# Five edits to the schedule of a windowed attention and feed-forward kernel: V's shift, one pair's casts, one pair's mask, the output copies and the last row group

## The chip, the cores and the metric

One core of a Trainium2 chip runs the whole program. The time is what the device needs for one execution, in microseconds (us). The kernel before took 345.44 us as the median of 4 runs (344.41 to 345.81). The core has five engines that run side by side, each with its own instructions in order: PE (matmuls; its weight loads are shown as PEld), DVE (vector work), ACT (activations and copies), POOL (also called GpSimd) and SP, which here only issues DMAs.

## What is computed

```python
def _attn_ref(q, k, v):                       # B, H, S, D = 8, 8, 576, 64
    scores = scale * np.matmul(q, k.transpose(0, 1, 3, 2))
    rel = pos[:, None] - pos[None, :]
    mask = (rel >= 0) & (rel < 64)
    scores = np.where(mask, scores, -1000000000.0)
    ...
    return np.matmul(attn, v)                 # attn: softmax of scores

def _moe_ref(x, w_in, w_out):                 # x: 4608 x 512
    h = x @ w_in                              # 512 x 2048
    g = h - np.tanh(h)
    return g @ w_out                          # 2048 x 512
```

Each query sees itself and the 63 keys ahead of it. The attention's output, with its heads side by side, is the input x of the second part. Inputs and output are float32; the kernel computes with bfloat16 operands and accumulates in float32.

## The kernel before

**Attention.** The 576 positions are cut into 9 windows of 64 queries; window j needs the 128 keys from 64 j - 64 to 64 j + 63. Heads are taken in pairs (h and h + 4), four pairs a batch, 32 pairs in all; pair g belongs to batch g // 4. A pair goes through these steps. Its q and k are loaded from DRAM by POOL's DMAs, rearranged by `cast` (two copies, `cast_pair` does both), transposed on PE (`tr_rows` or `tr`) and moved from PSUM to the tiles `kT` and `qs` or `qT`. `tile_scores` (pairs 0 to 9) or `scores` multiplies them for 5 and 4, or 3, windows at a time, and ACT writes the exponential into `PT`. `tile_pv` or `pv` multiplies with V, and DVE divides by the row sums into `xs`. `x_tr` (PE, then ACT or DVE) or `x_dma` transposes `xs` into `xT`, the operand of the second part.

**The mask** comes in two ways. With "hide", `hides` first adds a large negative number to the masked scores on PE, by a matmul of the identity with the tile `hide` for each head, before the scores are accumulated on top. With "mask", that is left out, and DVE multiplies the exponentials by the 0/1 tile `mask_sb` afterwards (line 278).

**V.** A batch's V is loaded, rearranged into `vb` by four copies (`cast_v`), and spread over the tile `vw` with one window of 64 keys in the upper 64 partitions of each column block: `keys_v`, 9 DMAs of 65 KB, issued in turn from POOL and SP. The lower 64 partitions are the same keys one block on. For the first three batches `shift_dve` copies them with two DVE instructions (line 154), for four blocks each; later ones use DMAs (`windows_v`, which writes a block's 128 keys at once, or `keys_v` with `shift_v`).

**The second part.** Tokens go in 9 chunks of 512. For each of 16 slices m of the hidden width, `hp_mm` does 4 matmuls (line 365, 128 x 512) into a PSUM bank and ACT takes the tanh; `g_sub` subtracts it on DVE into `gT`. For each group of 128 rows, `yp_mm` does 16 matmuls in four parts of four (line 389) into a bank, `y_out` copies the bank to SBUF on ACT (line 394) and issues the output DMA on SP (line 396).

**The order.** It is written out by hand. The last loop runs over half-steps h. `OPS` names the matmul part of a half-step: for chunk 0, slice m stands at h = 2 m; chunk 1 at 32 + 2 m; the output parts of chunk 0 at 64 + m; from h = 80 the slices of a chunk c stand at even h and the output parts of chunk c - 1 at odd h. `items` holds what else is given at a half-step: the attention's steps of the coming batches, in the order of the `at` calls. In a half-step the matmul part is given first, then the items, then `g_sub` of that slice. Every engine takes its instructions in the order in which they are given here.

The output copies are deferred: when a row group's fourth part is done (h = 67, 71, 75, 79, then each eighth odd half-step from 87 on), it is noted in `done`, and `flush` gives the copy and its DMA at the start of the next half-step that has a matmul part, after the items of its own:

```python
        if op:
            flush()
...
            yp_mm(*op[1:])
            if op[2] % 4 == 3:
                done.append((op[1], op[2] // 4))
```

The steps around the change, with the half-steps at which the kernel before gives them: pair 6's casts at 16, pair 7's at 18, both on DVE; pair 6's transposes at 17 and 18, its scores at 20 and 21; pair 7's transposes at 19 and 20, its scores at 23 and 24; batch 1's shift at 21 and its `tile_pv` at 22, 24, 26 and 28. On POOL: batch 2's `cast_v` at 21, its `keys_v`, both halves of w_out, q of batch 3, pair 9's casts, k and v of batch 3 all at 23, in this order, then pair 10's casts at 24 and pair 11's at 38. Pair 8's casts stand at 27 on DVE, its transposes at 29 and 30, its scores at 33 and 35. Batch 2's shift is at 40. Batch 3's V windows are issued at 71, four of them on SP and five on POOL.

PSUM banks: output groups use banks 0 and 1 in chunk 0, bank 2 in chunks 1 to 7, and banks 0 and 2 in turn in chunk 8, the last.

Of the kernel before, what the change touches and what calls it, by code (L numbers as in the profile page):

```python
# [7 lines left out]
F32 = mybir.dt.float32  # L8
BF16 = mybir.dt.bfloat16
ALU = mybir.AluOpType  # L10
ACT = mybir.ActivationFunctionType
# [4 lines left out]
def kernel(  # L16
# [9 lines left out]
    nc = tc.nc  # L26
# [5 lines left out]
    d_model = moe_w_in.shape[0]  # L32
    d_ff = moe_w_in.shape[1]
    NT = B * S
    TOK = 512
    WPC = TOK // 64
    NC = NT // TOK
    M = d_ff // 128
# [9 lines left out]
    sm_pool = ctx.enter_context(tc.tile_pool(name="sm", bufs=3))  # L48
# [6 lines left out]
    ps = psum.tile([128, 8, 512], F32, name="ps")  # L55
# [5 lines left out]
    mask = ps[:, 5, 448:480].bitcast(BF16)  # L61
    hide = const.tile([128, 2, 64], BF16, name="hide")
    WIDE = 1024, 1024
    w_in_sb = [const.tile([128, 4, n], BF16, name=f"wi{i}") for i, n in enumerate(WIDE)]
    w_out_sb = const.tile([128, M, d_model], BF16, name="w_out_sb")
# [76 lines left out]
    def cast_v(b, pr, eng=nc.gpsimd):  # L142
        move(eng, vb[:, :, 2 * pr:2 * pr + 2, 0:D].rearrange("p e h d -> p h e d"),
             stage.pop((b, pr, "v")).rearrange("p h (e d) -> p h e d", d=D))

    def keys_v(b, j, eng=nc.sync):

        eng.dma_start(out=vw[b % 2][64:128, j].rearrange("p h c -> p (h c)"),
                      in_=vb[8 * j:8 * j + 8].rearrange("p e h c -> p e (h c)"))
# [203 lines left out]
    gT = {}  # L353
# [5 lines left out]
    def hp_mm(c, ms, split):  # L359

        outs = [ps[:, hp_bank(c, m), :] for m in ms]
        for kis in ((0, 2), (1, 3)) if split else ((0, 1, 2, 3),):
            for m, hp in zip(ms, outs):
                for ki in kis:
                    nc.tensor.matmul(hp, w_in_tile(ki, m),  # L365
                                     chunk_tile(c)[:, :, ki % 2, 64 * (ki // 2):64 * (ki // 2) + 64],
                                     start=(ki == 0), stop=(ki == 3))
        for m, hp in zip(ms, outs):
            th = sm_pool.tile([128, TOK], F32, tag="th", name="th")
            nc.scalar.activation(th, hp, ACT.Tanh)  # L370
            HID[c, m] = hp, th

    def g_sub(c, m):
        hp, th = HID.pop((c, m))
        if m == 0:
            gT[c] = g_pool.tile([128, M, TOK], BF16, tag="gT", name="gT")
        nc.vector.tensor_tensor(gT[c][:, m, :], hp, th, ALU.subtract)  # L377

    def yp_bank(c, s):
        if c == 0:  # L380
            return s % 2
        return (0, 2)[s % 2] if c == NC - 1 else 2

    def yp_mm(c, st):
        s, part = divmod(st, 4)
        yp = ps[:, yp_bank(c, s), :]
        for i in range(4):
            m = 4 * part + i
            nc.tensor.matmul(yp, gT[c][:, m, s * 128:(s + 1) * 128], w_out_sb[:, m, :],  # L389
                             start=(m == 0), stop=(m == M - 1))  # L390

    def y_out(c, s):
        ysb = sm_pool.tile([128, d_model], F32, tag="ysb", name="ysb")
        nc.scalar.activation(ysb, ps[:, yp_bank(c, s), :], ACT.Copy)  # L394
        r0 = c * TOK + s * 128
        nc.sync.dma_start(out=out[r0:r0 + 128, :], in_=ysb)

    OPS = {}
    for m in range(M):
        OPS[2 * m] = "h", 0, m  # L400
        OPS[32 + 2 * m] = "h", 1, m
        OPS[64 + m] = "y", 0, m
        for c in range(2, NC + 1):
            if c < NC:
                OPS[32 * c + 16 + 2 * m] = "h", c, m
            OPS[32 * c + 17 + 2 * m] = "y", c - 1, m

    items = {}

    def at(h, fn, *args):  # L410
        items.setdefault(h, []).append((fn, args))

    done = []

    def flush():
        if done:
            y_out(*done.pop())

    def pace(h):

        c, m = [OPS[i][1:] for i in range(h) if OPS.get(i, "-")[0] == "h"][-1]
        nc.gpsimd.tensor_copy(tick, gT[c][0:1, m, 0:1])
# [5 lines left out]
    V, A, G, Y = nc.vector, nc.scalar, nc.gpsimd, nc.sync  # L428
# [75 lines left out]
        at(2, load, g, "q", G)  # L504
    at(16, cast_pair, 6, V)
    at(18, cast_pair, 7, V)
    at(21, shift_dve, 1, 0, 4)
    for g, t, ka, qa, a, b, eng in ((4, (10, 11, 13, 14), 6, 7, (4, 5), (6, 7), V),
                                    (5, (13, 14, 15, 15), 2, 3, (4, 5), (6, 7), V),
                                    (6, (17, 18, 20, 21), 2, 3, (4, 5), (4, 5), A),  # L510
                                    (7, (19, 20, 23, 24), 2, 3, (4, 5), (4, 5), A),
                                    (8, (29, 30, 33, 35), 3, 2, (4, 5), (4, 5), A),
                                    (9, (36, 37, 41, 43), 3, 2, (4, 5), (4, 5), A)):
        at(t[0], tr_rows, g, "k", ka, eng)
        at(t[1], tr_rows, g, "q", qa, A)
        at(t[2], tile_scores, g, 0, a, "hide" if g < 8 else "mask")
        at(t[3], tile_scores, g, 1, b, "hide" if g < 8 else "mask")
    for pr in range(NP):
        at(22 + 2 * pr, tile_pv, 4 + pr, (6, 7))
    at(27, x_tr, 1, 0, 0, 4, 3, A)  # L520
# [1 line left out]
    at(30, x_tr, 1, 1, 0, 4, 7, V)  # L522
    at(31, x_tr, 1, 1, 4, 9, 4, A)
    at(21, lambda: [cast_v(2, pr) for pr in range(NP)])
    at(27, cast_pair, 8, V)
    at(23, lambda: [keys_v(2, j, (G, Y)[j % 2]) for j in range(NJ)])
    at(23, load_w_out, 0)
    at(23, load_w_out, 1)
    at(23, load_all, 3, "q")
# [17 lines left out]
    for g in range(2 * NP + 2, B * NP):  # L547
        b, pr = divmod(g, NP)
        a = STEPS[b][pr] if b in STEPS else 8 * g - 36
# [34 lines left out]

    for h in range(32 * NC + 64):
        op = OPS.get(h)
        if op:
            flush()
        if op and op[0] == "h":
            c, m = op[1:]  # L590
            if c == 0 and m == 0:
                hp_mm(c, (0, 1, 2), True)
            elif c > 0 or m > 2:
                hp_mm(c, (m,), m == 0)
        elif op:
            yp_mm(*op[1:])
            if op[2] % 4 == 3:
                done.append((op[1], op[2] // 4))
        for fn, args in items.pop(h, []):
            fn(*args)  # L600
        if op and op[0] == "h":
            g_sub(*op[1:])
    flush()
    assert not items

# [28 lines left out]
```

The softmax here doesn't subtract the row's maximum and nothing guards it: scores larger than these inputs give would overflow.

## Time and profile before

| what | value |
|---|---|
| time of the profiled execution | 345.44 us |
| its span (first to last instruction) | 343.4 us |
| median of 4 runs | 345.44 us (344.41 to 345.81) |
| mean clock granted to PE | 0.970 of full speed |
| output matmuls (line 389) | 576, 144.2 us busy |
| slices' matmuls (line 365) | 576, 149.0 us busy |
| gT on DVE (line 377) | 144, 690 ns each |
| tanh on ACT (line 370) | 144, 599 ns each |
| output copies on ACT (line 394) | 36, 599 ns each |
| q and k casts on POOL (line 84) | 46, 855 and 833 ns mean |
| DMA bytes moved | 38.31 MB, mean 112 GB/s |

How to read it. Times are in us from the first instruction of one profiled execution unless marked ns. A row of a timeline gives start, length, engine, line of the kernel, operation, what it writes and reads with its shape, how many instructions were merged, and in brackets how long the engine stood idle just before and what ended that. A row of waits gives who waited for whom: total, times, longest. A row of stretches gives the window, its length, and for PE, PEld, DVE, ACT and POOL the busy time and number of instructions, then PE's granted clock, the busy share of the DMA engines, and GB/s. Matmuls are pipelined and their ends are modelled, so a busy PE need not be PE at its peak.

### The profile page before, as it was taken

To read this page: it belongs to the slowest core of one execution; us is meant where nothing else is said; L and a number is where in the kernel's file an instruction comes from. 1 tells how busy PE (TensorE), PEld (TensorE's weight loads), DVE (VectorE), ACT (ScalarE), POOL (GpSimd) and SP (SyncE) were. 2 spreads that over 40 slices of the span, in tenths; PEclk is the share of its full clock that TensorE was granted. 3 is DMA by queue.
4 is the path that set the end of the run, shared out by engine and by line. 5 is a ranking of instruction groups with operands and counts; after the bars stand their busy time and mean duration, and the time that the engine had idled before them with its cause. 6 is when DMAs were issued, how large, how long until landed. Compare 5 with 4: busy or idle time off the path is not lost.

```text
span 343.4 us, 6300 instructions
## 1 busy us (share of the span) xinstructions
PE 322.7 (94%) x2468; PEld 178.2 (52%) x2468; DVE 199.8 (58%) x330; ACT 188.7 (55%) x344; POOL 109.9 (32%) x158
## 2 busy tenths in 40 slices
PE   6687899889999999999999999999999999999995
PEld 2553555445555555655555555555555444444442
DVE  4476668877236766657676766666665444444300
ACT  3433787666366566666565666666653444444411
POOL 8933479603930815630823196100000000000000
PEclk9558999999999999999999999999999999999999
DMA  8999997993798289648694895433003200100021
GB/s 159 163 173 179 167 177 113 188 197 56 129 189 177 33 158 150 126 76 155 127 171 107 150 174 111 100 86 77 33 31 79 84 31 31 63 31 31 32 90 63
DMA packets 41245, 38.31 MB, mean 112 GB/s; under 512 B 13504, under 2 KB 34496, under 8 KB 41024
## 3 DMA queue, kind: packets, MB, share of 16 engines
q0 software_dynamic: 21296, 19.67, 38.6%
q1 hardware_dynamic: 19568, 17.82, 20.2%
q10 hardware_dynamic: 352, 0.43, 0.4%
q8 instruction: 19, 0.31, 0.4%
q14 instruction: 10, 0.08, 0.1%
HBM read 36.70 MB, written 9.44 MB: 134 GB/s over the span
## 4 chain that ended last, share of the span: by engine, by line
PE 76%; DMA 9%; DVE 7%; ACT 4%; POOL 2%; issue 2%; POOLq 0%; DVEq 0%; ACTq 0%
PE ps L389 36%; PE ps L365 29%; DMA vall<-in_v_dram 5%; PE ps L315 3%; PE ps L299 3%; PE ps L232 3%; DMA vw<-vb 2%; DVE gT L377 2%; DMA kall<-in_k_dram 2%; DVE xs L326 1%; DVE qt L84 1%; ACT ysb L394 1%; ACT qt L82 1%; POOL vall L126 1%; ACT th L370 1%
## 5 line engine op out<-in xcount | busy, mean ns | idle before, releaser
L365 PE MATMUL ps<-xT,wi 128*128 128x512 bf16 x576 | 149.0, 382 | 4.6 <-DVE gT L377 4.0
L389 PE MATMUL ps<-w_out_sb,gT 128*128 128x512 bf16 x576 | 144.2, 379 | 1.5 <-ACT ysb L394 1.5
L377 DVE TENSOR_TENSOR gT<-ps,th 128x512 bf16<-128x512 f32 x144 | 98.8, 690 | 76.7 <-ACT th L370 74.9
L370 ACT ACTIVATE th<-ps 128x512 f32<-128x512 f32 x144 | 86.0, 599 | 86.3 <-PE ps L365 83.2
L365 PEld LDWEIGHTS <-wi 128*128 128x128 bf16 x576 | 60.8, 114 | 51.2 <-issue 8.4
L389 PEld LDWEIGHTS <-gT 128*128 128x128 bf16 x576 | 53.4, 98 | 55.0 <-issue 2.8
L301 ACT ACTIVATE pt<-ps 128x384 bf16<-128x384 f32 x66 | 32.4, 491 | 24.6 <-PE ps L299 24.6
L84 POOL COPY vb<-vall 72x1024 bf16<-72x1024 bf16 x24 | 24.8, 1055 | 38.8 <-DMA vall<-in_v_dram 38.8
L326 DVE TENSOR_TENSOR xs<-ps,rc 64x576 bf16<-64x576 f32 x44 | 33.2, 755 | 1.1
L394 ACT ACTIVATE ysb<-ps 128x512 f32<-128x512 f32 x36 | 21.6, 599 | 18.2 <-PE ps L389 18.2
L84 DVE COPY qt<-ps 64x576 bf16<-64x576 bf16 x22 | 16.7, 760 | 25.4 <-ACT qt L82 25.3
L84 POOL COPY qb<-qall 96x768 bf16<-96x768 bf16 x23 | 19.7, 855 | 26.7 <-DMA qall<-in_q_dram 10.9
L315 PEld LDWEIGHTS <-pt 128*128 128x128 bf16 x198 | 16.6, 98 | 14.7
L315 PE MATMUL ps<-vw,pt 128*128 128x130 bf16 x198 | 22.0, 220 | 0.0
L299 PE MATMUL ps<-qt,kt 128*128 128x128 bf16 x198 | 21.8, 219 | 0.0
L299 PEld LDWEIGHTS <-kt 128*128 128x128 bf16 x198 | 15.4, 98 | 8.9 <-issue 0.3
L84 POOL COPY kb<-kall 96x768 bf16<-96x768 bf16 x23 | 19.1, 833 | 2.4 <-PE ps L232 2.4
L82 ACT ACTIVATE kt<-ps 128x576 bf16<-128x576 bf16 x26 | 16.9, 651 | 1.6 <-PE ps L232 1.5
L305 DVE TENSOR_TENSOR pt<-pt,ps 128x1152 bf16<-128x1152 bf16 x22 | 16.4, 745 | 0.8 <-ACT pt L301 0.8
L274 ACT ACTIVATE pt<-ps 128x640 bf16<-128x640 f32 (+1 forms) x20 | 12.5, 648 | 4.9 <-PE ps L271 4.8
L82 ACT ACTIVATE qt<-ps 64x576 bf16<-64x576 bf16 x22 | 14.0, 636 | 1.1 <-PE ps L232 1.1
L82 ACT ACTIVATE xT<-ps 128x512 bf16<-128x512 bf16 (+3 forms) x18 | 7.3, 456 | 8.3 <-PE ps L332 8.3
(72 smaller groups left out, 200.8 us busy)
## 6 DMA issues: line engine op xcount, KB each, us to landing
out_dram<-ysb SPq DMA_DIRECT2D x36, 256.0 KB
vall<-in_v_dram POOLq DMA_DIRECT2D x7, 576.0 KB, 13.0
qall<-in_q_dram POOLq DMA_DIRECT2D x5, 576.0 KB, 10.1
kall<-in_k_dram POOLq DMA_DIRECT2D x5, 576.0 KB, 10.2
vw<-vb SPq DMA_DIRECT2D x38, 65.0 KB
wi<-in_moe_w_in_dram POOLq DMA_DIRECT2D x2, 1024.0 KB, 16.5
w_out_sb<-in_moe_w_out_dram POOLq DMA_DIRECT2D x2, 1024.0 KB, 13.8
kall<-in_k_dram POOLq DMA_DIRECT2D x11, 144.0 KB, 7.6
```

The costliest lines, as they stand in the source:

```text
L82: nc.scalar.activation(o, i, ACT.Copy)
L84: eng.tensor_copy(o, i)
L299: nc.tensor.matmul(sp[:, i, :], kT[g % NR][:, 64 * j:64 * j + 128], qT[g % NR][:, :, 64 * j:64 * j + 64], start=True, stop=True)
L301: nc.scalar.activation(PT[g % NPT][:, 3 * grp:3 * grp + 3, :], sp, ACT.Exp, scale=scale)
L305: nc.vector.tensor_tensor(p, p, mask.unsqueeze(1).to_broadcast([128, 2 * NJ, 64]), ALU.mult)
L315: nc.tensor.matmul(ps[:, 5 + grp, 130 * i:130 * i + 130], PT[g % NPT][:, j, :], vw[b % 2][:, j, 2 * pr:2 * pr + 2, :], start=True, stop=True)
L326: nc.vector.tensor_tensor(xo[r, :, :, pr, :], ov[r, :, :, h, 0:D], rc[r].to_broadcast([64, 3, 3, 64]), ALU.mult)
L365: nc.tensor.matmul(hp, w_in_tile(ki, m), chunk_tile(c)[:, :, ki % 2, 64 * (ki // 2):64 * (ki // 2) + 64], start=(ki == 0), stop=(ki == 3))
L370: nc.scalar.activation(th, hp, ACT.Tanh)
L377: nc.vector.tensor_tensor(gT[c][:, m, :], hp, th, ALU.subtract)
L389: nc.tensor.matmul(yp, gT[c][:, m, s * 128:(s + 1) * 128], w_out_sb[:, m, :], start=(m == 0), stop=(m == M - 1))
L394: nc.scalar.activation(ysb, ps[:, yp_bank(c, s), :], ACT.Copy)
```

## The change

Five edits, given together:

1. Batch 1's shift on DVE is given at half-step 17, ahead of that half-step's transposes, instead of 21.
2. Pair 8's two casts move from DVE at 27 to POOL at 23, behind batch 2's `keys_v` and ahead of w_out's loads.
3. Pair 6's scores use the factor mask (DVE) instead of the added one (PE). Pairs 4, 5 and 7 keep the added one.
4. Output copies and their DMAs are given at once, right after the row group's last matmul and ahead of the half-step's items, instead of at the next matmul part.
5. The last group of 128 rows is computed by `y_last` in two halves of 256 columns, in banks 2 and 0, each with all 16 matmuls, a copy of its own and a DMA of its own.

```diff
@@ -395,6 +395,19 @@
         r0 = c * TOK + s * 128
         nc.sync.dma_start(out=out[r0:r0 + 128, :], in_=ysb)
 
+    def y_last():
+
+        c, s, n = NC - 1, 3, d_model // 2
+        for i in range(2):
+            yp = ps[:, 2 - 2 * i, 0:n]
+            for m in range(M):
+                nc.tensor.matmul(yp, gT[c][:, m, s * 128:(s + 1) * 128], w_out_sb[:, m, n * i:n * i + n],
+                                 start=(m == 0), stop=(m == M - 1))
+            ysb = sm_pool.tile([128, n], F32, tag="yhalf", name="yhalf")
+            nc.scalar.activation(ysb, yp, ACT.Copy)
+            r0 = c * TOK + s * 128
+            nc.sync.dma_start(out=out[r0:r0 + 128, n * i:n * i + n], in_=ysb)
+
     OPS = {}
     for m in range(M):
         OPS[2 * m] = "h", 0, m
@@ -409,12 +422,6 @@
 
     def at(h, fn, *args):
         items.setdefault(h, []).append((fn, args))
-
-    done = []
-
-    def flush():
-        if done:
-            y_out(*done.pop())
 
     def pace(h):
 
@@ -504,7 +511,7 @@
         at(2, load, g, "q", G)
     at(16, cast_pair, 6, V)
     at(18, cast_pair, 7, V)
-    at(21, shift_dve, 1, 0, 4)
+    at(17, shift_dve, 1, 0, 4)
     for g, t, ka, qa, a, b, eng in ((4, (10, 11, 13, 14), 6, 7, (4, 5), (6, 7), V),
                                     (5, (13, 14, 15, 15), 2, 3, (4, 5), (6, 7), V),
                                     (6, (17, 18, 20, 21), 2, 3, (4, 5), (4, 5), A),
@@ -513,8 +520,8 @@
                                     (9, (36, 37, 41, 43), 3, 2, (4, 5), (4, 5), A)):
         at(t[0], tr_rows, g, "k", ka, eng)
         at(t[1], tr_rows, g, "q", qa, A)
-        at(t[2], tile_scores, g, 0, a, "hide" if g < 8 else "mask")
-        at(t[3], tile_scores, g, 1, b, "hide" if g < 8 else "mask")
+        at(t[2], tile_scores, g, 0, a, "hide" if g in (4, 5, 7) else "mask")
+        at(t[3], tile_scores, g, 1, b, "hide" if g in (4, 5, 7) else "mask")
     for pr in range(NP):
         at(22 + 2 * pr, tile_pv, 4 + pr, (6, 7))
     at(27, x_tr, 1, 0, 0, 4, 3, A)
@@ -522,8 +529,8 @@
     at(30, x_tr, 1, 1, 0, 4, 7, V)
     at(31, x_tr, 1, 1, 4, 9, 4, A)
     at(21, lambda: [cast_v(2, pr) for pr in range(NP)])
-    at(27, cast_pair, 8, V)
     at(23, lambda: [keys_v(2, j, (G, Y)[j % 2]) for j in range(NJ)])
+    at(23, cast_pair, 8, G)
     at(23, load_w_out, 0)
     at(23, load_w_out, 1)
     at(23, load_all, 3, "q")
@@ -584,23 +591,22 @@
 
     for h in range(32 * NC + 64):
         op = OPS.get(h)
-        if op:
-            flush()
         if op and op[0] == "h":
             c, m = op[1:]
             if c == 0 and m == 0:
                 hp_mm(c, (0, 1, 2), True)
             elif c > 0 or m > 2:
                 hp_mm(c, (m,), m == 0)
-        elif op:
+        elif op == ("y", NC - 1, M - 4):
+            y_last()
+        elif op and op[1:] < (NC - 1, M - 4):
             yp_mm(*op[1:])
             if op[2] % 4 == 3:
-                done.append((op[1], op[2] // 4))
+                y_out(op[1], op[2] // 4)
         for fn, args in items.pop(h, []):
             fn(*args)
         if op and op[0] == "h":
             g_sub(*op[1:])
-    flush()
     assert not items
 
 # ---- launch: one core; inputs and outputs as the reference has them ----
```

## Prediction

> **What bounds the kernel now.** I read the page's engine table and its slices first, then PE's waits, then the stretches in a table, then the engines' timelines. "h" is the half-step of the schedule; "pair g" is a pair of heads, four pairs a batch.
>
> ```profile
> PE 322.7 (94%) x2468; PEld 178.2 (52%) x2468; DVE 199.8 (58%) x330; ACT 188.7 (55%) x344; POOL 109.9 (32%) x158
> PE   6687899889999999999999999999999999999995
> ...
> PE ps L365 <- DVE gT L377: 4.0, 8, 1.2
> PE ps L389 <- ACT ysb L394: 1.5, 4, 0.5
> PE ps L287 <- DVE vw L154: 0.8, 2, 0.6
> ...
> 40.00:60.00 20.00, 18.10 (x257) 10.66 (x257) 13.51 (x28) 15.57 (x29) 16.44 (x24) 1.00 0.89 137
> 200.00:220.00 20.00, 20.00 (x152) 11.55 (x151) 13.49 (x22) 12.65 (x24) 10.91 (x14) 1.00 0.66 126
> ```
>
> From 200 us on PE has no gap, so time lost or won before stays. PE can only be delayed or relieved in the gaps ahead of that, and after its last matmul. The change touches five places; these lines show them.
>
> ```profile
> 43.00 0.69 DVE L377 TENSOR_TENSOR gT<-ps,th 128x512 bf16<-128x512 f32 x1 [2.33 <-ACT th L370]
> 43.60 0.38 DVE L84 COPY kb<-kall 96x768 bf16<-96x768 bf16 x1
> 44.04 0.43 PE L252 MATMUL ps<-ident,kb 96*128 96x96 bf16 x6 [0.34 <-DVE kb L84]
> 46.73 1.31 DVE L154 COPY vw<-vw 64x2080 bf16<-64x2080 bf16 x2
> 49.37 4.03 POOL L84 COPY vb<-vall 72x1024 bf16<-72x1024 bf16 x4
> 53.70 2.93 POOL L148 DMA_DIRECT2D vw<-vb  x5 [0.30 <-POOL vb L84]
> 54.50 0.35 DVE L84 COPY kb<-kall 96x768 bf16<-96x768 bf16 x1
> 54.90 0.43 PE L252 MATMUL ps<-ident,kb 96*128 96x96 bf16 x6
> 59.67 1.38 DVE L278 TENSOR_TENSOR pt<-pt,mask_sb 128x640 bf16<-128x640 bf16 x1
> 64.12 2.05 DVE L154 COPY vw<-vw 64x2080 bf16<-64x2080 bf16 x2
> 115.81 0.61 ACT L394 ACTIVATE ysb<-ps 128x512 f32<-128x512 f32 x1
> 116.46 1.02 PE L389 MATMUL ps<-w_out_sb,gT 128*128 128x512 bf16 x4 [0.49 <-ACT ysb L394]
> 339.67 0.60 ACT L394 ACTIVATE ysb<-ps 128x512 f32<-128x512 f32 x1 [2.85 <-PE ps L389]
> 340.30 0.33 SPq L396 DMA_DIRECT2D out_dram<-ysb  x1
> ```
>
> In rows 2 and 3 PE already waits for pair 7's cast of k; row 8 follows row 7 with nothing between; the last four show a PE wait on an output copy and the tail.
>
> **The shift at h 17 instead of 21** (two DVE copies, no DMA). It moves ahead of pair 7's two casts and the gT of h 18. DVE is free at 43.00 + 0.69 = 43.69. The pair takes 1.31 (row 4) with POOL idle, and 1.66 at 18.03 us, where POOL issued DMAs, as it does at 43 us; I take 1.5. The cast of k, and PE's transposes in row 3, come some 1.4 us later (bounds 1.3 and 1.8). The shift must have batch 1's keys: POOL's DMAs of them were issued until 34.2 with 8.5 to 9.2 to landing, and at 39.1 with 3.4 to 3.7, so all are in by 43.4; SP's four show no landing, and with 9.2 after the last issue at 35.0 they would be in at 44.2, just in time for the second copy. What it won at h 21 is small: of PE's 0.8 us on vw, 0.55 stand at 66.22, another batch.
>
> **Pair 6 masked by a factor.** PE loses four matmuls with the identity, two pieces of 0.32 to 0.38 us in the chain; since the second one's successor still waits for the exponential that it waited for, I count 0.35 off PE. DVE gains two products, 0.48 and 0.42 us at 66.81 and 67.81; the first one is queued ahead of the gT of h 20, which moves from 46.01 to about 48.5. Its reader is the matmul of h 24, at 49.25 before and 50.3 now, so it lies in cover of about 1 us; without cover it would cost 0.9. After both parts PE is 1.05 us late (0.95 to 1.5).
>
> **Pair 8's casts on GpSimd.** DVE loses 0.35 and 0.36 us. On POOL they are queued behind four vb copies and five key DMAs, which hang on a DMA's landing at 48.5 and not on PE: 53.70 + 2.93 = 56.63. A POOL cast takes 0.83 and the next starts 0.77 later (58.84 and 59.61 before), so k is ready at 57.46 and q at 58.2. PE wants k at 54.90 + 1.05 = 55.95, and it is in order: it waits 1.5 us, and is late by 2.55 whatever the shift cost, as long as that is less. q is ready before the next four matmuls are through. Behind the casts on POOL everything moves 1.6 us: w_out (13.8 to landing, in by 74, first read 81.2), pair 9's casts (done at 61.3 and 62.1, wanted at 60.79 + 2.55), v of batch 3 (landed 82.5, now 84.1; its windows are read at 103.4). I count these as nothing.
>
> In return POOL's casts of pairs 9 to 11 lie 1 us earlier against DVE's work. The shift of batch 2 took 2.05 beside a POOL cast; starting near 66.7, with POOL done near 67, I take 1.45. DVE is what PE waits for there (0.55, 0.37 and 0.90 us at 66.2, 66.9 and 69.9), so 0.5 comes back. Bounds: nothing, and 1.6 if the mask in row 9 is shortened too and PE sees it all.
>
> The row on that: the mask with 640 elements took 1.38 us beside POOL casts and 0.48 alone. The Trainium skill (SBUF — State Buffer, Who interferes with whom) says a DVE operation with two SBUF inputs and a GpSimd read exclude each other, the second waiting for the whole of the first. By it pair 6's masks, near 49.4 us, would wait for a vb copy too, about 1 us that I don't count; the cover just takes it, and the sum would stay.
>
> **Output copies given at once.** A copy changes its place only where its half-step has other ACT work: h 79, 95, 111, 119, 135, 151. The four PE waits (0.49, 0.22, 0.30, 0.49, sum 1.5) belong to 95, 111, 135 and 151, where exponentials and transposes' copies stood ahead. They go, but the work behind the copy is 0.6 late: at 111 the xT copy that the first matmuls of chunk 3 wait for (0.15 back), at 79 pair 13's qt, whose PSUM bank PE takes again at 99.54, 0.14 after it was free (0.3 back). I take 1.0 of gain; bounds 1.5, and 0.4 if others are as tight. On SP's queue the output DMA of h 71 now goes ahead of four window DMAs that took 6.24 us to issue from 87.35. They wait for the copy, at 89.6 + 2.4, and end at 98.6; with the 7.8 us that POOL's windows took they land at 106.4, and are wanted at 105.9 + 2.4 = 108.3. Covered, by 1.9 us.
>
> **The last rows in two halves.** The last copy starts 0.07 after PE's end (339.60) and takes 0.60; 256 columns take 0.387 (xT's row of that width): 0.21 off. The last DMA moved its data from 341.0 to 341.97; half of it takes 0.49 by bytes, or as long by packets (128 both ways). Gain 0.2 to 0.7; I take 0.6. PE has 32 matmuls of 256 columns for 16 of 512, the same columns. Three weight loads with 130-column matmuls pass at 0.057 us each in the chain (0.17 for three), so the 16 more loads are hidden under 0.107 us of streaming. The Trainium skill speaks against this (TensorE: Matmul & The Clock Gate, The mechanism): loads overlap only with matmuls of another row group. By its price of 107 ns a load (same page, LDWEIGHTS) that would be 1.7 us more, and the sum 347.6; the rows show the overlap with all 128 rows in use, and the measurement decides.
>
> **Sum**, against the profiled execution: 345.44, of which 343.4 is span and 2.04 lies around it; it is also the median of the four runs (344.41 to 345.81). 345.44 + 2.55 - 0.5 - 1.0 - 0.6 = 345.9.
>
> **Rivals.** *The lateness is swallowed* (faster): PE's waits on DVE from 60 to 80 us sum to 2.9 us; if DVE free of two casts and of POOL gives back the 1.6, and the copies their full 1.5: 345.44 + 2.55 - 1.6 - 1.5 - 0.7 = 344.2. For it: both stretched DVE rows. Against it: POOL's casts are moved, not removed, and meet the mask at 61.58 instead. *GpSimd holds DVE* (slower): pair 8's second mask falls at 64.1 together with pair 10's cast and takes 1.3 instead of 0.44, and the shift stays at 2.05: 345.9 + 0.5 + 0.5 = 346.9. *SP's windows come too late* (slower): output copy ahead of the windows at h 71; it decides once the last window lands after 108.3. At 90 to 100 us the DMA engines are 0.95 busy and loads there took 12.5 to 17.4 us; with 12.5 it lands at 111.1, a wait of 2.8: 345.9 + 2.8 = 348.7. Against it: POOL's windows at the same time took 8.0 at most. *The copies change nothing* since what stood ahead was wanted just as early: 345.9 + 1.0 = 346.9.
>
> **How the numbers follow.** Forecast 0.40 (its own range 345.0 to 346.8), swallowed 0.22, GpSimd 0.20, windows 0.12, copies 0.06. About 0.3%, 1.04 us, is what a measurement of this kernel can tell from no change: 344.40 to 346.48. Faster: most of "swallowed" and a little of the forecast, 0.20. Slower: a fifth of the forecast, most of GpSimd's and the copies', all of the windows: 0.40. The range, 344.0 to 347.4, leaves out the windows and the tails.
>
> **What would show it.** Right: PE waits about 1.4 us on kb at pair 7's transposes and 1.5 on POOL's kb at pair 8's; no wait of PE on ysb before 200 us; a last copy near 0.39 us. Wrong: pair 8's casts on POOL ending before 56 us; PE waiting on vw DMAs near 106 us; a last group longer than 3.5 us on PE. I would be wrong most easily in the stretch from 58 to 72 us, where PE, ACT, DVE and POOL are all nearly full.

## The result, and the profile after

The changed kernel takes 346.25 us (median of 43 runs, 343.72 to 350.68), the kernel before 345.26 (median of 64, 342.79 to 352.76). The ratio is 1.0035, with a 95% interval of 1.0021 to 1.0049: 1.2 us more, where 0.5 were forecast. The ratios leave out runs that lie over 1.5% above the fastest of their kernel (3 of these 43, 10 of these 64), the medians are of all runs.

The profiled execution of the changed kernel took 343.72 us, the least of the 43, and has a span of 341.7 us, less than the 343.4 of the one before. So the two spans can't be subtracted, and this trace is not of a typical execution. Part of the difference lies ahead of everything that the change touches. Here are the stretches from 24 to 30 us, first before, then after; the third number from the right is PE's granted clock.

```profile
24.00:30.00 6.00, 5.77 (x31) 2.74 (x27) 2.50 (x5) 1.43 (x5) 0.65 (x1) 0.58 1.44 173
```

```profile
24.00:30.00 6.00, 5.26 (x37) 2.79 (x34) 3.21 (x7) 2.59 (x7) 1.15 (x2) 1.00 1.47 176
```

The same matmuls of chunk 0 ran at 0.58 of full speed in one execution and at full speed in the other. The gT of half-step 16, ahead of which nothing differs, starts at 43.00 before and at 41.74 after: 1.26 us that belong to the execution, not to the change. How much of it the clock made is open: in the profile of cast_only, below, the granted clock is 1.00 in this stretch too, and the same gT starts at 43.88. From that point on the two traces can be compared. PE's waits after:

```profile
PE ps L365 <- DVE gT L377: 4.0, 8, 0.9
PE ps L252 <- DVE kb L84: 1.9, 1, 1.9
...
PE ps L252 <- POOL kb L84: 0.7, 1, 0.7
...
PE ps L287 <- DVE vw L154: 0.4, 1, 0.4
```

The wait on ysb (1.5 us, four times) is gone. Two are there that were small or absent: on DVE's kb and on POOL's kb. The timeline after, at the places of the change:

```profile
41.74 0.69 DVE L377 TENSOR_TENSOR gT<-ps,th 128x512 bf16<-128x512 f32 x1 [2.30 <-ACT th L370]
42.46 1.41 DVE L154 COPY vw<-vw 64x2080 bf16<-64x2080 bf16 x2
43.90 0.36 DVE L84 COPY kb<-kall 96x768 bf16<-96x768 bf16 x1
44.31 0.43 PE L252 MATMUL ps<-ident,kb 96*128 96x96 bf16 x6 [1.86 <-DVE kb L84]
46.87 0.49 DVE L278 TENSOR_TENSOR pt<-pt,mask_sb 128x640 bf16<-128x640 bf16 x1 [1.75 <-ACT pt L274]
47.24 4.26 POOL L84 COPY vb<-vall 72x1024 bf16<-72x1024 bf16 x4
47.91 0.68 DVE L278 TENSOR_TENSOR pt<-pt,mask_sb 128x512 bf16<-128x512 bf16 x1
54.62 0.87 POOL L84 COPY kb<-kall 96x768 bf16<-96x768 bf16 x1
55.54 0.43 PE L252 MATMUL ps<-ident,kb 96*128 96x96 bf16 x6 [0.69 <-POOL kb L84]
...
336.83 0.39 ACT L407 ACTIVATE yhalf<-ps 128x256 f32<-128x256 f32 x1 [1.10 <-PE ps L404]
...
338.58 0.38 ACT L407 ACTIVATE yhalf<-ps 128x256 f32<-128x256 f32 x1 [1.36 <-PE ps L404]
```

Read against the rows before, with 1.26 added to each: pair 7's transposes are 1.53 us late (44.31 against 44.04), pair 8's 1.90 (55.54 against 54.90), and the first output matmul 1.17 (81.11 against 81.20). From there to the start of the last copy it took 338.58 - 81.11 = 257.47 against 339.67 - 81.20 = 258.47: 1.00 won. From that copy to the end of the span it took 341.7 - 338.58 = 3.12 against 343.4 - 339.67 = 3.73: 0.61 won. The account of these two traces closes: -1.26 + 1.17 - 1.00 - 0.61 = -1.70, the difference of the spans. Without the 1.26 it says 0.44 us less, where the runs say 1.2 more. So a typical execution loses more in the first 80 us than the 1.17 of this one.

### The profile page after: what moved, and what is told of

It reads as the page before. It is cut to its first block, busy times and chain, and to the rows that moved or that the text cites. A ratio compares the mean times of both kernels' runs of the same rounds, so it can differ in the third digit from the quotient of the medians.

```text
span 341.7 us, 6333 instructions
## 1 busy us (share of the span) xinstructions
PE 321.5 (94%) x2480; PEld 179.6 (53%) x2480; DVE 199.4 (58%) x330; ACT 189.2 (55%) x345; POOL 111.1 (33%) x160
## 4 chain that ended last, share of the span: by engine, by line
PE 75%; DVE 11%; ACT 6%; POOL 3%; issue 3%; DMA 2%; DVEq 0%; POOLq 0%; ACTq 0%
PE ps L389 33%; PE ps L365 30%; PE ps L315 3%; PE ps L299 3%; DVE gT L377 3%; PE ps L232 2%; DVE xs L326 2%; DMA kall<-in_k_dram 2%; ACT th L370 2%; DVE qt L84 2%; DVE vw L154 1%; ACT qt L82 1%; PE ps L404 1%; POOL vb L84 1%; PE ps L332 1%
## 5 line engine op out<-in xcount | busy, mean ns | idle before, releaser
L389 PE MATMUL ps<-w_out_sb,gT 128*128 128x512 bf16 x560 | 140.8, 379 | 0.0
L389 PEld LDWEIGHTS <-gT 128*128 128x128 bf16 x560 | 51.8, 98 | 51.0 <-issue 0.5
L84 POOL COPY kb<-kall 96x768 bf16<-96x768 bf16 x24 | 20.0, 833 | 1.3 <-PE ps L232 1.3
L148 POOL DMA_DIRECT2D vw<-vb x16 | 9.6, 605 | 6.3 <-DMA wi<-in_moe_w_in_dram 2.8
```

The costliest lines, as they stand in the source:

```text
L84: eng.tensor_copy(o, i)
```

## The experiments

Each kernel was timed against the kernel before on the same chip. "Before" and "changed" in the edits say from which of the two a kernel starts.

**Edits 4 and 5 alone** (late_only). Changed, with:

```diff
-    at(17, shift_dve, 1, 0, 4)
+    at(21, shift_dve, 1, 0, 4)
-        at(t[2], tile_scores, g, 0, a, "hide" if g in (4, 5, 7) else "mask")
+        at(t[2], tile_scores, g, 0, a, "hide" if g < 8 else "mask")
...
-    at(23, cast_pair, 8, G)
+    at(27, cast_pair, 8, V)
```

> Only edits 4 and 5 (output copies at once, last rows in two halves); shift, casts and mask as before. My theory: copies give 1.0 us and the tail 0.6, and nothing in the first 80 us pays for them, so 1.6 us less than the kernel before, a ratio of 0.995; in its profile no wait of PE on ysb. Rival (the copies only move their wait elsewhere, and the tail's DMA costs by packets): 0.2 us less, ratio 0.999. Rival (the later copies of qt and xT hold PE for as long as the output copies did, and the tail gains): ratio 0.998.

Measured: 0.9957 (0.9923 to 0.9991), 1.5 us less. PE's waits in its profile from 80 us on:

```profile
PE ps L232 <- DVE qt L84: 0.4, 1, 0.4
PE ps L365 <- DVE gT L377: 0.3, 1, 0.3
PE ps L332 <- DVE xs L326: 0.3, 1, 0.3
```

No ysb among them, and the waits that stay were there before. From its first output matmul (80.91) to the start of its last copy (338.37) it takes 257.46 us, as in the changed kernel. The interval is wide enough to hold the two rivals' 0.998 and 0.999 too, but the profiles of all kernels here decide: in the ten with edits 4 and 5 this stretch takes 257.4 to 257.6 us and the rest of the span 3.1 to 3.2, in the four without them 258.4 to 258.5 and 3.7. The copies' 1.0 and the tail's 0.6 stand.

**Edits 1 to 3 alone** (early_only). Changed, with:

```diff
+        if op:
+            flush()
...
-        elif op == ("y", NC - 1, M - 4):
-            y_last()
...
-                y_out(op[1], op[2] // 4)
+                done.append((op[1], op[2] // 4))
```

> Only edits 1 to 3 (shift at 17, pair 8's casts on GpSimd, pair 6's factor mask). My theory: 2.55 us of lateness at pair 8's transposes, 0.5 given back by 70 us: 2.05 us more than before, ratio 1.006. Rival (the lateness is swallowed between 58 and 72 us, where PE waits for DVE anyway): 0.5 us more or less, ratio 1.000 to 1.002. Rival (GpSimd's casts hold DVE): 3 us more, ratio 1.009.

Measured: 1.0104 (1.0060 to 1.0148), 6 runs, 3.6 us more. "Swallowed" falls. My theory's 1.006 is the lower end of the interval, and the rival's 1.009 lies inside it. Of that rival's two rows one came (pair 8's second product took 1.03 us for 0.44) and one didn't (batch 2's shift took 1.31, its length alone). The main loss in its profile is another:

```profile
50.40 4.03 POOL L84 COPY vb<-vall 72x1024 bf16<-72x1024 bf16 x4
54.73 2.86 POOL L148 DMA_DIRECT2D vw<-vb  x5 [0.30 <-POOL vb L84]
57.55 0.87 POOL L84 COPY kb<-kall 96x768 bf16<-96x768 bf16 x1
...
58.48 0.43 PE L252 MATMUL ps<-ident,kb 96*128 96x96 bf16 x6 [3.18 <-POOL kb L84]
```

V's load landed later here, the vb copies began at 50.40 instead of 49.37, and everything behind them on POOL moved with them. PE's wait for POOL is not one size. Of the six profiles of kernels with edit 2, four show it with 0.69, 1.58, 1.91 and 3.18 us, as V's landing falls against PE's progress, and two, those of undo_mask and after_psum, don't show it: there POOL's k was ready before PE came for it.

**Without edit 2** (undo_cast). Changed, with:

```diff
-    at(23, cast_pair, 8, G)
+    at(27, cast_pair, 8, V)
```

> The changed kernel with pair 8's casts back on DVE at half-step 27. My theory, in which PE waits at pair 8's transposes for GpSimd and the shift's cost hides under that wait: 1.05 us of early cost is left, 0.3 comes back, so with copies and tail 0.9 us less than before, ratio 0.9975; PE has no wait at pair 8's transposes (about 55 us). Rival (GpSimd has nothing to do with it, the shift is the cost): as the changed kernel, ratio 1.0035.

Measured: 1.0051 (1.0009 to 1.0093). Of its 12 runs three lie at 343.0 to 344.0, where I expected all, and eight at 347.2 to 349.1. My expectation failed, and the rival's reason too: the profiled execution (348.04) shows neither the wait for POOL nor that for the shift as its main loss, but this:

```profile
47.95 4.50 DVE L278 TENSOR_TENSOR pt<-pt,mask_sb 128x640 bf16<-128x640 bf16 x1 [2.62 <-ACT pt L274]
48.09 4.02 POOL L84 COPY vb<-vall 72x1024 bf16<-72x1024 bf16 x4
53.11 1.02 PE L365 MATMUL ps<-xT,wi 128*128 128x512 bf16 x4 [2.71 <-DVE gT L377]
...
58.25 0.87 POOL L84 COPY qb<-qall 96x768 bf16<-96x768 bf16 x1
58.32 1.68 DVE L84 COPY kb<-kall 96x768 bf16<-96x768 bf16 x1
...
60.06 0.43 PE L252 MATMUL ps<-ident,kb 96*128 96x96 bf16 x6 [1.30 <-DVE kb L84]
```

Pair 6's first product, 0.49 us elsewhere, took 4.50, until GpSimd had finished all four vb copies. The gT behind it on DVE came 4 us late, and PE waited 2.71 for it. This is edit 3, which I had put in cover, that is, in time in which PE waits for something else anyway. Such a stretching of a DVE instruction beside GpSimd's copies is called a hold from here on, and the four vb copies, given back to back, a train. A second, shorter one follows: pair 8's k, cast on DVE again, took 1.68 us instead of 0.35 beside a GpSimd cast, and PE waited 1.30 for it, where I expected no wait.

**Without edit 1** (undo_shift). Changed, with the shift back at 21.

> The changed kernel with the shift back at half-step 21. My theory: PE reaches pair 7's transposes 1.4 us sooner and then waits that much longer for GpSimd's cast at pair 8's, so the time stays near the changed kernel's, ratio 1.002 to 1.0035. Rival (the shift's 1.4 us is paid in full beside the cast's wait): 1.4 us less than the changed kernel, ratio 0.9995. Either way PE's wait of 1.9 us on DVE's kb at 44 us goes.

Measured: 1.0044 (1.0015 to 1.0073): the interval holds my theory's 1.002 to 1.0035, while the rival's 0.9995 is outside. PE's wait at pair 7's transposes shrinks to 0.30 us, and the one at pair 8's grows:

```profile
43.99 0.43 PE L252 MATMUL ps<-ident,kb 96*128 96x96 bf16 x6 [0.30 <-DVE kb L84]
...
56.62 0.87 POOL L84 COPY kb<-kall 96x768 bf16<-96x768 bf16 x1
...
57.55 0.43 PE L252 MATMUL ps<-ident,kb 96*128 96x96 bf16 x6 [1.91 <-POOL kb L84]
```

The earlier arrival is spent waiting for POOL. POOL's cast began at 56.62, where the prediction had put it at 56.63. That they meet so closely is luck: V landed here as it had in the profile before (the vb copies begin at 49.48, against 49.37), which it did not in others.

The next four were made to test the hold, as theory A, against theory B, cover.

**Without edit 3** (undo_mask). Changed, with `"hide" if g < 8`.

> The changed kernel with pair 6's added mask back on PE (two DVE products less). Theory A (pair 6's products on DVE read two tiles in SBUF and are held by GpSimd's four vb copies in most runs, 4.5 us in the one profile that caught it): without them no hold can come; PE's wait for GpSimd's kb at pair 8's transposes stays, about 2 us late, so 0.3 to 0.6 us less than the changed kernel, ratio to before 1.002. Theory B (the products are in cover): 0.35 us more on PE, swallowed by the wait for GpSimd: ratio 1.0035, as the changed kernel.

Measured: 1.0021 (0.9994 to 1.0049). That is A's number, but B's is inside the interval: not told apart by the time. The wait of about 2 us for POOL that A left in place isn't in the profile.

**Without edit 2, the mask from PSUM** (undo_cast_psum), and **the change with the mask from PSUM** (after_psum). In both, the products of pair 6 take as factor the PSUM copy that the kernel keeps for the later pairs:

```diff
-            nc.vector.tensor_tensor(p, p, mask_sb.unsqueeze(1).to_broadcast([128, 2 * n, 64]), ALU.mult)
+            factor = mask if g in (6,) else mask_sb
+            nc.vector.tensor_tensor(p, p, factor.unsqueeze(1).to_broadcast([128, 2 * n, 64]), ALU.mult)
```

> The changed kernel with pair 8's casts back on DVE, and pair 6's two products taking the mask from its copy in PSUM instead of the one in SBUF: one source in SBUF is left. Theory A (two SBUF sources meet GpSimd's copies): the product near 48 us takes 0.5 us however it meets them, the times of 347 to 348 that undo_cast showed in two thirds of its runs are gone, and the ratio is 0.998 (undo_cast: 1.005). Theory B (the four vb copies hold any DVE instruction on SBUF, or the 4.5 us came from something else at that time): still 347 to 348 in most runs, ratio 1.005.

> The changed kernel with the mask from PSUM for pair 6 alone. Theory A: no hold; what is left is PE's wait for GpSimd's kb at pair 8's transposes, with copies and tail 0 to 0.5 us more than before, ratio 1.000 to 1.0015. Theory B: as the changed kernel, 1.0035.

Measured: 1.0012 (0.9985 to 1.0039) and 1.0016 (0.9990 to 1.0042). The first lies under undo_cast and rules out B's 1.005, but A's 0.998 is just outside its interval too: five of its 12 runs still lie over 347.3, so the product is not the only thing that can cost 4 us. What it was in these is open. The second lies close to A's range, but B's 1.0035 is inside its interval, and the wait for POOL that A left in place isn't in its profile. The row says more than the time (this kernel's products stand at line 279):

```profile
48.75 4.02 POOL L84 COPY vb<-vall 72x1024 bf16<-72x1024 bf16 x4
49.47 0.42 DVE L279 TENSOR_TENSOR pt<-pt,ps 128x512 bf16<-128x512 bf16 x1 [0.49 <-ACT pt L274]
```

Inside the train the product with one SBUF source takes 0.42 us, its ordinary length.

**Edits 4 and 5 with pairs 8 and 9 from PSUM** (late_psum). As above with `g in (8, 9)`, on top of late_only.

> Edits 4 and 5 alone, and pairs 8's and 9's products with the mask from PSUM. Theory A: the product at 59.7 us, which took 1.38 and 0.99 us in two profiles, takes 0.5; PE waits 0.2 us less there, ratio 0.995 against 0.9957 without it. Theory B: no difference, 0.9957. In both faster than the kernel before and than the changed one.

Measured: 0.9977 (0.9953 to 1.0001). No gain, and A's 0.995 is outside. The product at 58.28 takes 0.48 us, as A said, but PE now waits on it:

```profile
PE ps L271 <- DVE pt L279: 1.6, 2, 1.3
```

The mask lies in PSUM bank 5, into which the next scores go, so they wait until the product has read it. One wait was exchanged for another.

**Edit 2 alone** (cast_only) and **edit 1 alone** (shift_only), each on the kernel before.

```diff
-    at(27, cast_pair, 8, V)
+    at(23, cast_pair, 8, G)
```

> The kernel before with edit 2 alone (pair 8's casts on GpSimd behind batch 2's keys). My theory: POOL's kb is there some 2.5 us after PE wants it, PE waits that long at pair 8's transposes near 55 us, and 0.5 comes back by 70 us: 2.0 us more, ratio 1.006. Rival (swallowed): the wait is there, but the time is within 0.5 us of before, ratio 1.000 to 1.0015.

> The kernel before with edit 1 alone (shift at 17). My theory: PE waits 1.7 to 1.9 us at pair 7's transposes near 44 us (0.3 before), 0.2 comes back at the first PV matmuls: 1.2 us more, ratio 1.0035. Rival (it is regained by 70 us, since DVE is freed at half-step 21): ratio 1.000.

Measured: 1.0045 (1.0011 to 1.0078) and 1.0026 (1.0001 to 1.0050), 1.6 and 0.9 us, with PE's waits of 1.58 on POOL's kb and 1.78 on DVE's kb. My theories' 1.006 and 1.0035 are inside. The rivals' 1.000 lies outside both intervals, just so for the second; the upper end of the first rival, 1.0015, does not.

**The hold made likely** (mask7_sbuf, mask7_psum). On late_only, pair 7 instead of pair 6 is masked by the factor, so that its products should fall inside the vb copies; the second kernel takes the factor from PSUM.

```diff
-        at(t[2], tile_scores, g, 0, a, "hide" if g < 8 else "mask")
+        at(t[2], tile_scores, g, 0, a, "hide" if g < 7 else "mask")
```

> Edits 4 and 5 alone, plus pair 7 (instead of 6) masked by the factor from SBUF, so that its two products fall at 49.4 to 51.5 us, in the middle of GpSimd's four vb copies (49.0 to 53.0 in late_only). Theory A (a product with two SBUF sources waits for GpSimd): a product takes 2 to 4.5 us in the profile, PE waits 1 to 3 us on DVE near 52 us, ratio to before 1.000 to 1.004 (late_only: 0.9957). Theory B (no hold): 0.5 us each, ratio 0.995 to 0.996.

> As mask7_sbuf, with the mask from its copy in PSUM for pair 7: the same products at the same place with one SBUF source. Theory A: 0.5 us each beside the same vb copies; PE may wait up to 0.7 us for the product's read of the PSUM bank; ratio 0.996 to 0.998. Theory B: as mask7_sbuf, whatever that is.

Measured: 1.0000 (0.9963 to 1.0037) with a median of 347.29, against 0.9964 (0.9943 to 0.9985) with a median of 344.00. Eight of 12 runs of the first lie at 346.0 to 350.0, one of 9 of the second over 345; of late_only, from which both start, it is four of 12 over 345. Both ratios are theory A's. The rows of mask7_sbuf:

```profile
50.07 4.02 POOL L84 COPY vb<-vall 72x1024 bf16<-72x1024 bf16 x4
...
50.96 3.82 DVE L278 TENSOR_TENSOR pt<-pt,mask_sb 128x640 bf16<-128x640 bf16 x2
...
55.82 0.51 PE L287 MATMUL ps<-vw,pt 128*64 128x65 bf16 x20 [3.61 <-DVE xs L293]
```

Two products that take 0.9 us elsewhere end at 54.78, 0.7 after the last vb copy; the first of them alone took 3.48. What they held up on DVE reaches PE as a wait of 3.61 us. The profile of mask7_psum, of its longest execution (350.51), doesn't show the counterpart: there DVE came to the products only at 56.34 and 58.08, behind the train. So the row of after_psum is the only one with a whole product from PSUM inside a train.

## Why the prediction came out as it did

**The sum.** 345.9 was forecast, 346.25 is the median. The gains of 1.6 us were right in size and cause. The early loss was put at 2.05 us (2.55 less 0.5); the difference of the ratios of the changed kernel and late_only, 1.0035 and 0.9957, makes it about 2.7, uncertain by over 1 us. Single executions say less: measured from the gT of half-step 16 to the first output matmul, the loss is 1.17 in the profile of after and 4.47 in that of early_only (84.93 - 42.26 against 81.20 - 43.00). So it is in part luck that a figure from one trace of the kernel before came so near.

**Shift.** Right: 1.4 us was the price at pair 7's transposes, 1.53 was measured (the pair of copies took 1.41 beside POOL's DMA issues, for the 1.5 taken). All keys had landed; DVE did not wait. Alone it costs 0.9 us (0.0 to 1.7).

**Casts on GpSimd.** The mechanism is right wherever PE comes first, in four of the six profiles: PE waits for POOL's kb, the time is set by V's landing and not by PE, and the shift's cost hides under it (undo_shift). The term was 2.55 for both steps. In the profile of after it was 1.90, since V landed 2.1 us sooner there while PE was 1.26 ahead; k's cast ended at 55.49, before the 56 that the prediction had named as a sign of being wrong. In other executions PE waited up to 3.18, or not at all. One execution gave one value of a quantity that moves by 3 us between executions, and the prediction treated it as fixed.

**What comes back.** 0.5 was forecast, 0.73 was measured between pair 8's transposes and the first output matmul (1.90 to 1.17). In the profile of early_only nothing came back: 4.32 at the transposes, 4.47 at the matmul. Batch 2's shift took 1.51 us instead of 2.05, as read from the order on POOL. The rival that GpSimd holds pair 8's second product is right as to the row (1.00 us for 0.44), but it did not decide.

**Pair 6's mask.** This step holds in one execution and fails in another. The prediction gave PE 0.35 us and put the two products under 1 us of cover, "about 1 us that I don't count; the cover just takes it". In the profiled execution of after it went about so: the second product came to DVE at 47.91, inside the first vb copy (47.24 to 48.30), and was through at 48.59; the second copy took 1.26 us, the other three 1.05 to 1.07. The rows of undo_cast and mask7_sbuf show the other case: there a product with two sources in SBUF waited not for one vb copy but until the last of the train had ended, up to 4.5 us, which no cover takes. What decides between the two is not shown, and how often the long hold strikes the changed kernel was not traced. Its size can be bounded only loosely: the change without edit 3 stands at 1.0021, with the mask from PSUM at 1.0016, the change itself at 1.0035, which is 0.5 to 0.7 us between middles whose intervals overlap. It has the size and the sign of the 0.7 us by which the forecast was too low; that it accounts for them is possible, not shown, and longer waits for POOL would do it too. Edit 3 was not run alone. With the Trainium skill's rule (SBUF — State Buffer, Who interferes with whom), that the two engines exclude each other, the traces agree in kind, and the product in after, through after one copy, in length too; a wait through four operations rather than one is the runs' own.

**Copies.** Right: 1.0 us, 1.00 measured. All four waits, 1.5 us, went, and the 0.5 that the prediction took off for work behind the copies was needed. Its larger part stands where the prediction put it, at 0.3: PE's transposes at 99.54 come at 99.73, which is 0.28 later against the first output matmul (99.73 - 81.11 against 99.54 - 81.20). A wait of 0.28 on gT at 165.08 is new too, and was not forecast.

**Tail.** Right: 0.6, 0.61 measured. PE's two halves cost what the row of weight loads promised: the two last copies start 1.75 us apart, for 16 matmuls of 256 columns, so 3.50 for the group, against 3.45 between the last two copies before (336.22 and 339.67). The row of PE for the group, 3.66 us, is over the 3.5 that the prediction set as a limit, but it has a modelled end in it. By the prediction's estimate from the Trainium skill's rule that loads overlap only with matmuls of another row group (TensorE: Matmul & The Clock Gate, The mechanism), the group would have been 1.7 us longer; these rows don't agree with it.

**Rivals.** The window DMAs behind an output copy on SP were no cost: after has no wait of PE on vw near 106 us. "The copies change nothing" falls with late_only. "Swallowed" falls with early_only.

## What to carry to other kernels

An engine whose work hangs on a DMA's landing and one whose work hangs on PE's progress drift against each other from run to run (in the profiles here the vb copies begin at 46.8 to 50.4 us, the gT of half-step 16 at 41.6 to 45.1); a step moved from the second to the first is not priced by one trace, and moving it early in program order doesn't make it early. Before a DVE product with two SBUF sources is put near GpSimd copies, look at the whole train of copies, not at one. Of five edits given together, two gained 1.5 us and the other three together lost more: only the output copies at once and the split last rows should stay, at 0.9957 of the time before (0.9923 to 0.9991), the lowest ratio here.

## What the hardware showed unexpectedly

A hold can last through back-to-back GpSimd copies: one product took 4.50 us and two took 3.82 beside trains of 4.02. It need not: the product of 0.68 in after was through after one copy of its train, and pair 8's second product, beside two GpSimd casts, took 1.00 us in the same profile, for 0.44 before. Nor is it confined to products. In the profiled execution of mask7_psum batch 1's shift, two DVE copies that take 1.31 us alone, met such a train:

```profile
48.83 5.41 DVE L154 COPY vw<-vw 64x2080 bf16<-64x2080 bf16 x2
...
49.66 4.02 POOL L84 COPY vb<-vall 72x1024 bf16<-72x1024 bf16 x4
...
54.29 0.42 PE L288 MATMUL ps<-vw,pt 128*64 128x65 bf16 x10 [3.67 <-DVE vw L154]
```

That shift stands at half-step 21, where the kernel before has it. At 17 it ran at 42.46 to 43.87, 3.4 us ahead of the train. Whether edit 1 keeps the shift out of such meetings in a useful share of executions was not tried; against it stands the 0.9 us that it costs in the others.
